# Reordering the loads of a fused attention and FFN block over two DMA queues

## The chip, the cores and the metric

One core of a Trainium2 chip runs the whole kernel. The metric is the device time of one execution in microseconds (us), lower is better. The core's engines are TensorE (PE, matmuls; PEld is its loading of weights), VectorE (DVE), ScalarE (ACT), GpSimd (POOL) and SyncE (SP). DMAs are issued from SP and ACT, each with its own queue; 16 DMA engines move the bytes of both.

## What is computed

x has 2048 rows of 512 in bf16; F is 1792; there are 32 heads of 16.

```python
xn = _layernorm(x, axis=-1)
return x + _A_ref(xn, A_wqkv, A_wo) + _B_ref(xn, B_w_gate, B_w_up, B_w_down)
# A: linear attention
q, k, v = heads of (xn @ wqkv)
phi = lambda t: jnp.where(t > 0, t + 1, jnp.exp(t)) + 1e-6
kv = einsum("bhsd,bhse->bhde", phi(k), v);  z = sum of phi(k) over s
o = (phi(q) @ kv) / (phi(q) . z + 1e-6);    A = o @ wo
# B: the FFN
B = (silu(xn @ w_gate) * (xn @ w_up)) @ w_down
```

## The kernel before

The rows are handled as 16 tiles of 128 rows (x0 to x15). Everything stays in SBUF: x, the normalized xn, its transpose xnT, and all weights.

First stage, tile by tile: statistics of x (`stat`, lines 277 to 303: two DVE instructions and two small ones, most on POOL), xn on DVE (`xn_dve`, line 285; tile 0 in two halves, line 328), the transpose of xn into xnT, then K's and Q's projections on PE (`proj`, line 365; tile 0 in halves of the contraction, `proj_half`, line 378), their exponentials on ScalarE (lines 401 to 411), K's features on DVE (`feat_k`: a clip, line 418, and a max-and-add from PSUM, line 427), and the accumulation of the features' transpose with xn (`gtacc`, line 460). Tiles 0 to 3 are transposed on PE (lines 340 and 312); tiles 4 to 15 by a DMA transpose on SP (`transpose_dma`, line 356), issued behind each tile's xn. K of tile t writes PSUM bank 2(t mod 2) and Q of tile t the bank after it, so K of tile 2 needs the bank of K of tile 0, which `feat_k(0)` reads last.

Second stage, FFN steps j = 0 to 55 (`ffn`, line 568): four matmuls with w_gate, four with w_up, Silu on ScalarE, a product on DVE. Between them stand `kvt` (reads w_v, line 666, after j = 1), `mmat` (reads w_o, line 689, after j = 3), the column sums z (`z_split`, `z_cols` with two DMA transposes, line 616, `z_sum`, line 623), the division by the attention's denominator, and from j = 17 on the output tiles (`outtile`), which read w_down (line 751).

The order of work on each engine is the order in which the program emits it, and it is written out by hand. `_Prog` derives the semaphore waits from named resources: an operation waits for the writers of what it reads. Every DMA has a semaphore of its own, and a DMA that must wait holds up everything behind it on its issuing queue. The weights of Q, K and V are one tensor of 512 rows; `wqkv_load(eng, h, name, i, c0, n)` (line 198) loads n row blocks of 128 (c0 to c0 + n - 1) of one of the three, and its name in the resources is (name, c0). `xload` (line 192) loads n tiles of x from t0. `wpiece` (line 211) loads one row block of w_gate or w_up (448 KB), `wload` (line 208) a whole weight.

Loads before, in the order of issue:

- SP: x0, x1, x2, K's blocks 0-1, Q's blocks 0-1, x4, x5, then, after Q's weights have landed, x6 to x9, x10 and x11, x12 to x15.
- ACT: K's blocks 2-3, x3, Q's blocks 2-3.
- SP, among the transposes: a piece of w_gate in each of the loop steps t = 2, 4, 6, 8 (line 539); w_up's four pieces, w_v and w_o at t = 11 (lines 541 to 544); w_down at t = 14 (line 546). xn of tiles 14 and 15, with their transposes, is emitted at t = 9.

PE starts with matmuls on a constant (`fill`, line 249), which have no result that is used.

Of the kernel before, what the change touches and what calls it, by code (L numbers as in the profile page):

```python
# [17 lines left out]
NDC = D // P  # L18
# [90 lines left out]
def bass_parallel_sum__linear_attn_block__swiglu_ffn__prompt_kernel(  # L109
# [13 lines left out]
    pe, act, dve, pool, sp = nc.tensor, nc.scalar, nc.vector, nc.gpsimd, nc.sync  # L123
    bf, f32 = dt.bfloat16, dt.float32

    with contextlib.ExitStack() as es:
        E = es.enter_context

        def sb(name, shape, d=bf):
            return E(nc.sbuf_tensor(name, [P] + shape, d))  # L130
# [3 lines left out]
        xnT = sb("xnT", [NDC, S])  # L134
        wqkv_sb = sb("wqkv_sb", [NDC, 3 * D])
        wo_sb = sb("wo_sb", [NG, D])
        wg_sb = sb("wg_sb", [NDC, F])
        wu_sb = sb("wu_sb", [NDC, F])
        wd_sb = sb("wd_sb", [NFC, D])
# [45 lines left out]
        def bk(i):  # L185
            return ("bank", i)
# [5 lines left out]
        def xload(eng, h, t0, n, after=()):  # L192
            K.dma(
                eng, lambda: h.dma_start(x_sb[:, t0:t0 + n, :], xv[:, t0:t0 + n, :]),
                r=list(after), w=[("x", t0 + i) for i in range(n)],
            )

        def wqkv_load(eng, h, name, i, c0, n):
            K.dma(
                eng,  # L200
                lambda: h.dma_start(
                    wqkv_sb[:, c0:c0 + n, i * D:(i + 1) * D],
                    A_wqkv[c0 * P:(c0 + n) * P, i * D:(i + 1) * D].rearrange("(c p) f -> p c f", p=P),
                ),
                w=[(name, c0)],
            )

        def wload(eng, h, name, dst, src):
            K.dma(eng, lambda: h.dma_start(dst[:, :, :], src.rearrange("(c p) f -> p c f", p=P)), w=[(name,)])

        def wpiece(name, dst, src, c):
            K.dma("sp", lambda: sp.dma_start(dst[:, c, :], src[c * P:(c + 1) * P, :]), w=[(name, c)])
# [1 line left out]
        K.op("pool", lambda: pool.memset(warm[:, :], 0.0), w=[("warm",)])  # L214
        K.op("act", lambda: act.activation(warm[:, :], warm[:, :], ACT.Exp), r=[("warm",)], w=[("warm",)])
        xload("sp", sp, 0, 1)
        xload("sp", sp, 1, 1)
        xload("sp", sp, 2, 1)
        wqkv_load("sp", sp, "wk", 1, 0, 2)
        wqkv_load("act", act, "wk", 1, 2, 2)  # L220
        xload("act", act, 3, 1)
        wqkv_load("sp", sp, "wq", 0, 0, 2)
        wqkv_load("act", act, "wq", 0, 2, 2)
        xload("sp", sp, 4, 1)
        xload("sp", sp, 5, 1)
        xload("sp", sp, 6, 4, [("wq", 0), ("wq", 2)])
        xload("sp", sp, 10, 2)
        xload("sp", sp, 12, 4)

# [8 lines left out]
            r=[("ident",)], w=[("ident",)],  # L238
# [16 lines left out]
        def masks():  # L255
            K.op("pool", lambda: pool.memset(maskt[:, :], 1.0), w=[("mask",)])
            mview = maskt[:, :].rearrange("p (a b) -> p a b", a=P // DH)
            K.op(
                "pool",
                lambda: pool.affine_select(  # L260
                    out=mview, in_=mview, compare_op=ALU.is_ge, fill=0.0,
                    base=0, pattern=[[-DH, P // DH], [0, DH]], channel_multiplier=1,
                ),
                r=[("mask",)], w=[("mask",)],
            )
            K.op(
                "pool",
                lambda: pool.affine_select(
                    out=mview, in_=mview, compare_op=ALU.is_ge, fill=0.0,
                    base=DH - 1, pattern=[[DH, P // DH], [0, DH]], channel_multiplier=-1,  # L270
                ),
                r=[("mask",)], w=[("mask",)],
            )
# [87 lines left out]
        def proj(t, b, lo, wname):  # L361
            K.op(
                "pe",
                [
                    (lambda c=c: pe.matmul(  # L365
                        banks[b], xnT[:, c, t * P:(t + 1) * P], wqkv_sb[:, c, lo:lo + D],
                        start=(c == 0), stop=(c == NDC - 1),
                    ))
                    for c in range(NDC)
                ],  # L370
                r=[("xnT", t), (wname, 0), (wname, 2)], w=[bk(b)],
            )

        def proj_half(t, b, lo, wname, h):
            K.op(
                "pe",
                [
                    (lambda c=c: pe.matmul(
                        banks[b], xnT[:, c, t * P:(t + 1) * P], wqkv_sb[:, c, lo:lo + D],
                        start=(c == 0), stop=(c == NDC - 1),  # L380
                    ))
                    for c in (2 * h, 2 * h + 1)
                ],
                r=[("xnTh", t, h), (wname, 2 * h)], w=[bk(b)],
            )

        def kb(t):
# [5 lines left out]
        def kproj(t):  # L393
            proj(t, kb(t), D, "wk")

        def qproj(t):
            proj(t, qb(t), 0, "wq")

        def exp_k(t):
            K.op(  # L400
                "act", lambda: act.activation(ek[:, t % NE, :], banks[kb(t)], ACT.Exp),  # L401
                r=[bk(kb(t))], w=[("ek", t % NE)],
            )

        def exp_q(t):
            K.op(
                "act", lambda: act.activation(eq[:, t, :], banks[qb(t)], ACT.Exp),
                r=[bk(qb(t))], w=[("eq", t)],
            )
            K.op(  # L410
                "act", lambda: act.activation(pkq[:, t, 1, :], banks[qb(t)], ACT.Copy),  # L411
                r=[bk(qb(t))], w=[("pq", t)],
            )
# [19 lines left out]
        def feat_k(t):  # L433
            e = t % NE
            clip(ek[:, e, :], ("ek", e))
            if t >= 2:
                zsum(t - 2, e)
            maxadd(pkq[:, t, 0, :], banks[kb(t)], ek[:, e, :], [bk(kb(t)), ("ek", e)], [("pk", t)])
# [17 lines left out]
        def gtacc(t):  # L456
            K.op(
                "pe",
                [
                    (lambda c=c: pe.matmul(  # L460
                        banks[4 + c], xn_sb[:, t, c * P:(c + 1) * P], pkq[:, t, 0, :],
                        start=(t == 0), stop=(t == NT - 1),
                    ))
                    for c in range(NDC)
                ],
                r=[("xn", t), ("pk", t)], w=[bk(4 + c) for c in range(NDC)],
            )

        def stat(t):
            bns(t)  # L470
            agg(t)
            rstd_pow(t)

        def xn(t):
            xn_dve(t)
            if t >= 4:
                transpose_dma(t)
# [49 lines left out]
        for t in range(2, NT):  # L527
            if t >= 3:
                kproj(t)
                exp_k(t)  # L530
                qproj(t)
                exp_q(t)
                feat_k(t)
            for i in STAT.get(t, ()):
                stat(i)
            for i in XN.get(t, ()):
                xn(i)
            if t in (2, 4, 6, 8):
                wpiece("wg", wg_sb, B_w_gate, t // 2 - 1)
            if t == 11:  # L540
                for c in range(NDC):
                    wpiece("wu", wu_sb, B_w_up, c)
                wqkv_load("sp", sp, "wv", 2, 0, 4)
                wload("sp", sp, "wo", wo_sb, A_wo)
            if t == 14:
                wload("sp", sp, "wd", wd_sb, B_w_down)
            if t == 12:
                masks()
            if t >= 3:
                gtacc(t - 2)  # L550
# [53 lines left out]
        def z_split():  # L604
            K.op("pool", lambda: pool.tensor_copy(zhi[:, :], zacc[:, :]), r=[("zacc",)], w=[("zhi",)])
            K.op(
                "pool",
                lambda: pool.tensor_tensor(out=zlo[:, :], in0=zacc[:, :], in1=zhi[:, :], op=ALU.subtract),
                r=[("zacc",), ("zhi",)], w=[("zlo",)],
            )  # L610

        def z_cols():
            for i, (src, name) in enumerate(((zhi, "zhi"), (zlo, "zlo"))):
                K.dma(
                    "sp",
                    lambda i=i, src=src: sp.dma_start_transpose(out=zT[:, i, :, :], in_=src[:, :]),
                    r=[(name,)], w=[("zT", i)],
                )
# [36 lines left out]
        def z_rows():  # L655
            K.op(
                "pool",
                lambda: pool.tensor_tensor(out=zb[:, :], in0=zrow[:, 0, :], in1=zrow[:, 1, :], op=ALU.add),
                r=[("zrow", 0), ("zrow", 1)], w=[("zb",)],
            )  # L660
# [125 lines left out]
            gt_evac(c)  # L786
        z_split()
        z_cols()
        NORM0 = 9
        PE_OUT = {3: 0, 6: 1, 9: 2, 12: 3}  # L790
        for j in range(NJ):
# [7 lines left out]
            if j == 4:  # L799
                z_sum()  # L800
            if j == NORM0 - 1:
                z_rows()
            if NORM0 <= j < NORM0 + 3 * NT:
                i, ph = (j - NORM0) // 3, (j - NORM0) % 3
                if ph == 0:
# [40 lines left out]
```

## Time and profile before

| what | us |
|---|---|
| median of three runs | 214.52 |
| the three runs | 214.17, 214.52, 217.59 |
| the profiled execution | 214.81 |
| its span (first to last instruction) | 213.6 |
| PE busy in the span | 207.7 |
| DVE, ACT, POOL busy | 119.2, 67.7, 72.6 |

The difference between the profiled execution and its span, 1.2 us, lies around the program. In a timeline each line has the start, the time, the engine, the line of the kernel, the operation, what is written and read, the tile's shape and how many instructions are merged; a bracket tells how long the engine was idle before it and which event ended that. Times are us from the start of the span. In the DMA view a line has what is loaded, the issuing queue, the number of issues, the KB of each and the median us from issue to landing; asked for a stretch with one issue in it, it gives that issue's own. The granted TensorE clock is full (1.00) in every stretch of the profile.

### The profile page before, as it was taken

Reading aid. Unit: us, or ns where it says so; the run is one execution under the profiler, and the core shown is the slowest. Engines: PE = TensorE matmul, PEld = TensorE weight load, DVE = VectorE, ACT = ScalarE, POOL = GpSimd, SP = SyncE. Lnnn points to the kernel's source line nnn. Section 1 sums busy time; section 2 is a strip of 40 time slices with the busy share of each in tenths; the row PEclk is TensorE's granted clock in tenths of the full one; section 3 lists DMA queues with packets and bytes.
Section 4 is the critical chain, followed back from the end, with each engine's and each line's share of the span. In section 5 each row is a group of like instructions: output and inputs, shape, how many; then the busy total and the mean of one; then the engine's idle time right before and its main releaser. Section 6 shows DMA issues by size and latency. Waiting matters only on the chain.

```text
span 213.6 us, 2768 instructions
## 1 busy us (share of the span) xinstructions
PE 207.7 (97%) x985; PEld 96.9 (45%) x1004; DVE 119.2 (56%) x240; ACT 67.7 (32%) x118; POOL 72.6 (34%) x95
## 2 busy tenths in 40 slices
PE   8799999999999999999999999999999999999995
PEld 4344434444544444444444444444444444444454
DVE  3799986333553777446373755464656536364121
ACT  2486666667363332213021302122132213121000
POOL 2538885549014344042130442121414131221100
PEclk9999999999999999999999999999999999999999
DMA  5784797997202011101101021101011010110101
GB/s 177 257 205 127 137 156 167 291 369 237 49 0 52 0 25 25 49 17 35 25 26 49 3 26 48 49 0 49 3 49 25 25 25 28 49 25 28 49 28 51
DMA packets 26271, 16.19 MB, mean 76 GB/s; under 512 B 18064, under 2 KB 24848, under 8 KB 26256
## 3 DMA queue, kind: packets, MB, share of 16 engines
q1 hardware_dynamic: 25568, 15.34, 28.5%
q10 hardware_dynamic: 688, 0.66, 1.0%
q8 instruction: 8, 0.13, 0.3%
q14 instruction: 7, 0.06, 0.1%
HBM read 9.70 MB, written 2.10 MB: 55 GB/s over the span
## 4 chain that ended last, share of the span: by engine, by line
PE 84%; issue 0%; DVE 0%
PE psum L568 45%; PE psum L751 23%; PE psum L740 6%; PE psum L365 6%; PE psum L460 4%; PE psum L666 0%; PE psum L689 0%; DVE out_sb L764 0%
## 5 line engine op out<-in xcount | busy, mean ns | idle before, releaser
L583 ACT ACTIVATE sg<-psum 128x512 bf16<-128x512 f32 x56 | 33.4, 598 | 106.8 <-PE psum L568 104.9
L568 PE MATMUL psum<-xnT,wu_sb 128*128 128x512 bf16 x222 | 57.4, 379 | 0.1
L568 PE MATMUL psum<-xnT,wg_sb 128*128 128x512 bf16 x217 | 56.0, 379 | 0.4
L698 POOL TENSOR_TENSOR prod<-pkq,zb 128x512 f32<-128x512 bf16 x16 | 18.6, 1161 | 57.8 <-DVE pkq L427 57.8
L568 PEld LDWEIGHTS psum<-xnT,wu_sb 128*128 128x128 bf16 x224 | 21.9, 98 | 26.4
L568 PEld LDWEIGHTS psum<-xnT,wg_sb 128*128 128x128 bf16 x224 | 21.9, 98 | 26.2
L764 DVE TENSOR_TENSOR out_sb<-psum,x_sb 128x512 bf16<-128x512 f32 (+1 forms) x17 | 11.2, 660 | 36.1 <-PE psum L751 36.1
L589 DVE TENSOR_TENSOR pkq<-psum,sg 128x512 bf16<-128x512 f32 x28 | 19.2, 687 | 18.6 <-PE psum L568 14.1
L722 POOL TENSOR_TENSOR pqn<-pkq,rden 128x512 bf16<-128x512 bf16 x16 | 16.9, 1055 | 36.6 <-DVE rden L716 36.6
L365 PE MATMUL psum<-wqkv_sb,xnT 128*128 128x512 bf16 x118 | 28.4, 379 | 0.5 <-ACT pkq L411 0.3
L589 DVE TENSOR_TENSOR xn_sb<-psum,sg 128x512 bf16<-128x512 f32 x28 | 18.8, 671 | 14.2 <-PE psum L568 13.6
L751 PE MATMUL psum<-wd_sb,xn_sb 128*128 128x512 bf16 (+1 forms) x124 | 25.6, 355 | 0.1
L751 PE MATMUL psum<-wd_sb,pkq 128*128 128x512 bf16 x110 | 25.4, 379 | 0.1
L452 POOL TENSOR_TENSOR zacc<-zacc,pkq 128x512 f32<-128x512 f32 x15 | 17.3, 1153 | 7.6 <-DVE ek L418 7.3
L365 PEld LDWEIGHTS psum<-wqkv_sb,xnT 128*128 128x128 bf16 x120 | 11.4, 98 | 14.4 <-ACT pkq L411 0.8
L751 PEld LDWEIGHTS psum<-wd_sb,xn_sb 128*128 128x128 bf16 x126 | 12.3, 98 | 11.9
L751 PEld LDWEIGHTS psum<-wd_sb,pkq 128*128 128x128 bf16 x112 | 11.0, 98 | 13.2
L740 PE MATMUL psum<-m_sb,eq 128*128 128x512 bf16 (+1 forms) x66 | 16.2, 366 | 0.1
L460 PE MATMUL psum<-pkq,xn_sb 128*128 128x512 bf16 x62 | 15.8, 379 | 0.1
L706 DVE TENSOR_REDUCE den<-prod 128x32 f32<-128x512 f32 x16 | 10.9, 684 | 5.7 <-POOL prod L698 5.7
L277 DVE BATCH_NORM_STATS2 stats<-x_sb 128x6 f32<-128x512 bf16 x16 | 10.9, 682 | 3.6 <-DMA x_sb<-in_A_x_dram 3.6
L401 ACT ACTIVATE ek<-psum 128x512 bf16<-128x512 f32 x16 | 9.6, 598 | 9.4 <-issue 4.1
(56 smaller groups left out, 131.4 us busy)
## 6 DMA issues: line engine op xcount, KB each, us to landing
out_dram<-out_sb SPq DMA_DIRECT2D x15, 128.0 KB, 1.7
wg_sb<-in_B_w_gate_dram SPq DMA_DIRECT2D x4, 448.0 KB, 4.2
wu_sb<-in_B_w_up_dram SPq DMA_DIRECT2D x4, 448.0 KB, 4.8
wd_sb<-in_B_w_down_dram SPq DMA_DIRECT2D x1, 1792.0 KB, 13.5
x_sb<-in_A_x_dram SPq DMA_DIRECT2D x2, 512.0 KB, 4.5
x_sb<-in_A_x_dram SPq DMA_DIRECT2D x5, 128.0 KB, 3.9
wqkv_sb<-in_A_wqkv_dram ACTq DMA_DIRECT2D x2, 256.0 KB, 4.0
wqkv_sb<-in_A_wqkv_dram SPq DMA_DIRECT2D x2, 256.0 KB, 5.5
```

What stands on the lines that cost most here:

```text
L277: K.op("dve", lambda: dve.bn_stats(stats[:, t, :], x_sb[:, t, :]), r=[("x", t)], w=[("st", t)])
L365: (lambda c=c: pe.matmul(banks[b], xnT[:, c, t * P:(t + 1) * P], wqkv_sb[:, c, lo:lo + D], start=(c == 0), stop=(c == NDC - 1),))
L452: lambda: pool.tensor_tensor(out=zacc[:, :], in0=zacc[:, :], in1=pk, op=ALU.add),
L460: (lambda c=c: pe.matmul(banks[4 + c], xn_sb[:, t, c * P:(c + 1) * P], pkq[:, t, 0, :], start=(t == 0), stop=(t == NT - 1),))
L568: (lambda c=c: pe.matmul(banks[b], w_sb[:, c, fc * P:(fc + 1) * P], xnT[:, c, C * 512:(C + 1) * 512], start=(c == 0), stop=(c == NDC - 1),))
L583: lambda: act.activation(sg[:, j % NSG, :], banks[gb], ACT.Silu),
L589: lambda: dve.tensor_tensor(out=hT(C, fc), in0=banks[ub], in1=sg[:, j % NSG, :], op=ALU.mult,),
L698: lambda: pool.tensor_tensor(out=p, in0=pkq[:, t, 1, :], in1=zb[:, :], op=ALU.mult),
L722: lambda: pool.tensor_tensor(out=pqn[:, t % NPN, :].rearrange("p (h e) -> p h e", e=DH), in0=pkq[:, t, 1, :].rearrange("p (h e) -> p h e", ...
L740: (lambda g=g: pe.matmul(dst, pqnT(t)[:, g, :], m_sb[:, g, lo:hi], start=(g == 0), stop=False,))
L751: (lambda fc=fc: pe.matmul(dst, hT(C, fc)[:, jj * P:(jj + 1) * P], wd_sb[:, fc, lo:hi], start=False, stop=(fc == NFC - 1),))
L764: lambda: dve.tensor_tensor(out=o, in0=src, in1=x_sb[:, t, lo:hi], op=ALU.add),
```

## The change

The first eleven loads are dealt over both queues in another order. SP: x0, x2, K's blocks 2-3, x3, Q's block 3, x4, and, after all of Q's weights have landed, x6 to x9, then x10 and x11, x12 to x15 as before. ACT: x1, K's blocks 0-1, Q's blocks 0-1, Q's block 2, x5. Q's blocks 2 and 3 are now two loads, so the readers of Q's weights wait for both. All pieces of w_gate, then w_up, w_v and w_o are issued at t = 9, behind the transposes of tiles 14 and 15. w_down is issued after z's two transposes.

```diff
         xload("sp", sp, 0, 1)
-        xload("sp", sp, 1, 1)
+        xload("act", act, 1, 1)
         xload("sp", sp, 2, 1)
-        wqkv_load("sp", sp, "wk", 1, 0, 2)
-        wqkv_load("act", act, "wk", 1, 2, 2)
-        xload("act", act, 3, 1)
-        wqkv_load("sp", sp, "wq", 0, 0, 2)
-        wqkv_load("act", act, "wq", 0, 2, 2)
+        wqkv_load("act", act, "wk", 1, 0, 2)
+        wqkv_load("sp", sp, "wk", 1, 2, 2)
+        wqkv_load("act", act, "wq", 0, 0, 2)
+        xload("sp", sp, 3, 1)
+        wqkv_load("act", act, "wq", 0, 2, 1)
+        wqkv_load("sp", sp, "wq", 0, 3, 1)
         xload("sp", sp, 4, 1)
-        xload("sp", sp, 5, 1)
-        xload("sp", sp, 6, 4, [("wq", 0), ("wq", 2)])
+        xload("act", act, 5, 1)
+        xload("sp", sp, 6, 4, [("wq", 0), ("wq", 2), ("wq", 3)])
         xload("sp", sp, 10, 2)
         xload("sp", sp, 12, 4)
...
-                r=[("xnT", t), (wname, 0), (wname, 2)], w=[bk(b)],
+                r=[("xnT", t), (wname, 0), (wname, 2)] + ([(wname, 3)] if wname == "wq" else []), w=[bk(b)],
...
-                r=[("xnTh", t, h), (wname, 2 * h)], w=[bk(b)],
+                r=[("xnTh", t, h), (wname, 2 * h)] + ([(wname, 3)] if wname == "wq" and h else []), w=[bk(b)],
...
-            if t in (2, 4, 6, 8):
-                wpiece("wg", wg_sb, B_w_gate, t // 2 - 1)
-            if t == 11:
+            if t == 9:
+                for c in range(NDC):
+                    wpiece("wg", wg_sb, B_w_gate, c)
                 for c in range(NDC):
                     wpiece("wu", wu_sb, B_w_up, c)
                 wqkv_load("sp", sp, "wv", 2, 0, 4)
                 wload("sp", sp, "wo", wo_sb, A_wo)
-            if t == 14:
-                wload("sp", sp, "wd", wd_sb, B_w_down)
...
         z_split()
         z_cols()
+        wload("sp", sp, "wd", wd_sb, B_w_down)
```

## The prediction

> **What bounds the kernel now.** I read the page's busy line first, then the chain that ended last, then the timeline of TensorE (PE) alone from the start to the FFN, then the stretches where that row of matmuls is broken: the timeline of all engines from 0 to 16 us, and the DMA issues one at a time with their time to landing.
>
> ```profile
> span 213.6 us, 2768 instructions
> PE 207.7 (97%) x985; PEld 96.9 (45%) x1004; DVE 119.2 (56%) x240; ACT 67.7 (32%) x118; POOL 72.6 (34%) x95
> ...
> PE 84%; issue 0%; DVE 0%
> ```
>
> PE is busy in 207.7 of 213.6 us, and the chain is PE from 30.43 us to the last tile. Only a hole between matmuls can be won, and only a new hole can be lost. The timeline of PE has two holes that data makes:
>
> ```profile
> 6.08 0.48 PE L249 MATMUL psum<-const-bfloat16-1.0 128*128 128x128 bf16 x4
> 7.73 1.02 PE L378 MATMUL psum<-wqkv_sb,xnT 128*128 128x512 bf16 x4 [1.17 <-DMA wqkv_sb<-in_A_wqkv_dram]
> 8.59 0.39 PE L312 MATMUL psum<-ident,xn_sb 128*128 128x128 bf16 x4
> 8.81 1.03 PE L378 MATMUL psum<-wqkv_sb,xnT 128*128 128x512 bf16 x4
> 9.68 1.03 PE L365 MATMUL psum<-wqkv_sb,xnT 128*128 128x512 bf16 x4
> ...
> 27.41 1.89 PE L365 MATMUL psum<-wqkv_sb,xnT 128*128 128x512 bf16 x8
> 29.14 1.03 PE L460 MATMUL psum<-pkq,xn_sb 128*128 128x512 bf16 x4
> 30.48 1.89 PE L365 MATMUL psum<-wqkv_sb,xnT 128*128 128x512 bf16 x8 [0.32 <-ACT pkq L411]
> ```
>
> Hole one: the first real projection, K of tile 0, starts at 7.73 us, 1.17 us after the last filler, and waits for K's weights. From there PE runs without a gap: groups of four matmuls follow each other every 0.86 us. Call 7.73 T0; whatever moves T0 moves the end.
>
> Hole two: the tile groups start every 2.59 us (24.82, 27.41), but the next at 30.48 instead of 30.00: 0.48 us lost. The row names ScalarE, but that write (Q of tile 8) is not what K of tile 9 needs. The DMA view shows what it needs, xn's transpose of tile 9, issued at 24.09 us behind a piece of w_gate at 23.13:
>
> ```profile
> 24.09 1.19 SPq L356 DMA_TRANSPOSE xnT<-xn_sb  x1
> ```
> ```profile
> xnT<-xn_sb SPq DMA_TRANSPOSE x1, 6.3
> ```
>
> 24.09 + 6.3 = 30.4, which is when PE goes on. Transposes with no weights ahead of them (issues at 14.05, 16.89, 21.89, 32.11) land in 2.4 us.
>
> **The start, part by part.** The first stage is a race of 1,792 KB. Landings before, each issue plus its own latency, with the KB that its queue had then delivered: SP x0 3.0 (128), x1 4.4 (256), x2 5.6 (384), K's rows c 0-1 7.6 (640), Q's c 0-1 8.26 (896), x4 8.6 (1,024), x5 9.0 (1,152); ACT K's c 2-3 4.0 (256), x3 5.2 (384), Q's c 2-3 6.7 (640). Between 4.0 and 6.7 us, both queues busy, ACT's moved 384 KB in 2.7 us; from 4.4 to 7.6 SP's moved 384 KB in 3.2.
>
> After, SP carries x0, x2, K's c 2-3, x3, Q's c 3, x4 (896 KB); ACT carries x1, K's c 0-1, Q's c 0-1, Q's c 2, x5 (896 KB). Same bytes, 11 issues in place of 10. The split of Q's second half adds one issue of about 0.45 us (those rows last 0.40 to 0.49) on ACT's queue, which has five now; they end near 3.3 us and ScalarE's first evacuation is at 6.06, so that is hidden. By position:
> - x1 first on ACT's queue: about 3.2 instead of 4.4.
> - K's c 0-1 at ACT's 384 KB: 5.2 instead of 7.6. K's c 2-3 at SP's 512 KB: 6.6 (halfway from 5.6 to 7.6).
> - Q's c 0-1 at ACT's 640: 6.7. x3 at SP's 640: 7.6 (before 5.2, so later by 2.4). Q's c 2 and 3, which end at 1,536 KB over both queues, where Q's c 0-1 stood before: 8.3. x4 among the last 256 KB: 8.9, between x4's 8.6 and x5's 9.0 before.
>
> Now the wait that takes over. T0 must satisfy:
> - the first xnT. Without K's weights PE is free at 6.56. VectorE (DVE) would do x1's statistics 0.33 us earlier, and the halves of xn(0) behind them, so 6.2 to 6.5.
> - K's c 2-3 are used 0.43 us after T0: 6.6 - 0.4 = 6.2.
> - Q's c 2 and 3 are first used 1.5 us after T0 (0.86 + 0.22 + 0.43): 8.3 - 1.5 = 6.8.
> - x3 and x4 sit in DVE's queue ahead of the features of tile 0:
>
> ```profile
> 8.65 0.69 DVE L277 BATCH_NORM_STATS2 stats<-x_sb 128x6 f32<-128x512 bf16 x1 [0.30 <-DMA x_sb<-in_A_x_dram]
> ...
> 9.38 0.18 DVE L280 BATCH_NORM_AGGREGATE mv<-stats 128x2 f32<-128x6 f32 x1
> ...
> 10.13 0.29 DVE L418 TENSOR_SCALAR ek<-ek 128x512 bf16<-128x512 bf16 x1 [0.57 <-ACT ek L401]
> ...
> 10.46 0.69 DVE L427 SCALAR_TENSOR_TENSOR pkq<-psum,ek 128x512 bf16<-128x512 f32 x1
> ```
>
> The reader is to see that DVE already waits 0.30 us for x4 here. The 0.57 us wait for K's exponential goes when T0 comes earlier. Then x4's landing plus 0.95 (statistics) plus 1.02 (clip to the end of line 427) is x4 + 2.0. K of tile 2 writes the same bank and starts 3.91 us after T0 (11.64 before): T0 is at least 8.9 + 2.0 - 3.9 = 7.0. x3's chain (0.69 + 0.1 + 0.41 to the end of xn(2), then x4's statistics, then the same 2.0) gives 7.6 + 3.2 - 3.9 = 6.9.
>
> So T0 becomes 7.0: a gain of 0.73 of the 1.17 us; late next is x4, with Q's last rows beside it. Bounds for x4: 8.57, if nothing but the same bytes counts (T0 6.66, gain 1.07); and 640 KB past x1's old place at SP's rate of 384 KB in 3.2 us, 4.4 + 5.3 = 9.7 (T0 7.8, a loss of 0.1). I take 8.9, since the total does not grow. The outer end, if x4 is no gate, is the first bullet's 6.4: gain 1.3. The wait ahead of x6's load now names Q's c 3 too; behind it on SP stand x10, x12 and the transpose of tile 4. Before, they were released at 8.2 to 8.3, as Q's weights landed: the same 8.3 now. x6 landed at 11.7 and was read past 13, so 1.3 us of cover.
>
> **The weights, part by part.** Moving four pieces of w_gate (issues of 0.58 us at 18.13, 23.13, 27.95, 33.34) behind the transposes gives hole two back: 0.48 us. [...]
>
> What it costs: w_gate (landed by 37.2, read at 50.1) joins one burst. In the burst of before, w_up's first piece was issued at 36.79 and landed after 3.9 us, and 10.3 pieces' worth (w_up, w_v, w_o, w_down) had landed by 53.6: 1.39 us a piece past the first. Now w_gate and w_up are first, eight pieces: 3.9 + 7 x 1.39 = 13.6 us after the first issue (12.1 at 1.17 a piece, 14.3 at 1.49, the fastest and slowest rows). That issue follows the transpose of tile 15, so it moves with PE, and so does the first read of w_up at 51.0: cover is 51.0 - 36.79 = 14.2 us. It fits by 0.6; I put nothing, at the slow end 0.1. w_v lands 1.5 later, 15.1, read at 53.6 (16.8); w_o 16.7 against 57.9 (21.1). w_down, issued behind z's two transposes near 54, takes at most its old 13.5 and is read at 83.8; if that cover were gone each us late would be one lost. z's transposes ran beside w_down before and still landed in 2.4. SP loses nothing: its issues are fewer between transposes.
>
> Sum: 0.73 + 0.48 = 1.2 us. The profiled execution took 214.81 us (span 213.6), 0.3 above the median of 214.52; its span should become 212.4, and the median 214.5 - 1.2 = 213.3.
>
> **The rivals.**
> - *The start gives nothing.* x3, Q's rows or x4 come so late that T0 stays at 7.6 to 7.9. For it: the 16 DMA engines are full from 2.5 to 7.5 us in both orders, and x3 is later by 2.4 us. Against: K's first rows jump from 7.6 to 5.2. Only hole two goes: 214.0.
> - *All of the start.* x4 lands before 8.3, T0 is 6.4: gain 1.33 + 0.48, 212.7. Against: x4's 8.57 before, with the same bytes ahead.
> - *w_up is late* (slower). It begins to cost when the eighth piece lands more than 14.2 us after the first issue and outweighs the 1.2 us gained past 15.4, which is 1.64 us a piece. At 1.9 us a piece it is 17.2: 3.0 lost, net 1.8 slower, 216.3. Against: no row of the old burst is over 1.49. For: it is the only cover under 1 us.
> - *The change does nothing to hole two*, because the transposes of tiles 9 to 11 hold each other (three in 2.5 us landed at 30.4, 30.7, 31.2): 213.8. It counts within the forecast's case.
>
> **How the numbers follow.** Forecast 0.62, nothing from the start 0.20, all of the start 0.11, w_up late 0.07. The forecast's own range is 212.9 to 214.0 (its x4 bounds with hole two in or out). Repeats lie 0.3 either side, so 212.4 to 214.7 takes in the second and third case too and leaves out the late w_up and some odd run. A measurement of this kernel can tell about 2% (4.3 us) from no change; no case here gains that, and w_up would need 2.2 us a piece to lose it: faster 0.02, same 0.94, slower 0.04.
>
> **What would show it.** Right: the first projection near 7.0 us or at 6.4 with small waits behind it; DVE's statistics of tile 3 and 4 waiting for x; groups every 2.59 us through tile 9; no transpose over 4 us after 18 us; no wait at the first w_up matmul. Wrong: x4 landing past 9.5 or before 8.3, a PE wait on a DMA near 49 us, or transposes of tiles 9 to 11 still landing late.

## The result, and the profile after

The changed kernel took 213.22 us (median of 13 runs, 212.96 to 214.0), the kernel before beside it 214.84 us (13 runs, 214.17 to 217.59). The ratio is 0.9928, 95% interval 0.9907 to 0.9948: 1.5 us faster, within 2%. The times of the kernel before fall in two groups, nine at 214.2 to 215.0 and four at 215.7 to 217.6 us, those of the changed kernel in one; the experiments take the second group up. The ratio is that of the means without the run at 217.59 us; against the lower group alone the mean of the changed kernel is 1.24 us lower.

The page of the profiled execution after (213.49 us) begins:

```profile
span 212.3 us, 2770 instructions
...
PE 207.1 (98%) x985; PEld 96.2 (45%) x1004; DVE 119.2 (56%) x240; ACT 68.0 (32%) x118; POOL 72.7 (34%) x95
```

The span is 1.3 us shorter. PE's timeline, the same rows as before:

```profile
6.46 1.02 PE L379 MATMUL psum<-wqkv_sb,xnT 128*128 128x512 bf16 x4
7.33 0.39 PE L313 MATMUL psum<-ident,xn_sb 128*128 128x128 bf16 x4
7.55 0.59 PE L379 MATMUL psum<-wqkv_sb,xnT 128*128 128x512 bf16 x2
8.42 0.59 PE L379 MATMUL psum<-wqkv_sb,xnT 128*128 128x512 bf16 x2 [0.28 <-DMA wqkv_sb<-in_A_wqkv_dram]
...
9.94 0.81 PE L366 MATMUL psum<-wqkv_sb,xnT 128*128 128x512 bf16 x3
11.08 1.02 PE L366 MATMUL psum<-wqkv_sb,xnT 128*128 128x512 bf16 x4 [0.33 <-DVE pkq L428]
...
13.03 1.03 PE L461 MATMUL psum<-pkq,xn_sb 128*128 128x512 bf16 x4
...
26.84 1.89 PE L366 MATMUL psum<-wqkv_sb,xnT 128*128 128x512 bf16 x8
...
29.43 1.89 PE L366 MATMUL psum<-wqkv_sb,xnT 128*128 128x512 bf16 x8
...
49.29 1.03 PE L567 MATMUL psum<-xnT,wg_sb 128*128 128x512 bf16 x4
50.20 1.02 PE L567 MATMUL psum<-xnT,wu_sb 128*128 128x512 bf16 x4
```

The first projection starts at 6.46 us, 1.27 earlier. Two waits give part of it back: Q's second half runs at 8.42 instead of 7.98 (0.44 lost), and K of tile 2 at 11.08 instead of 10.80 (0.28 lost), behind line 428 on DVE. At the first accumulation (13.03, before 13.59) 0.56 us is left. Hole two is gone: 26.84 and 29.43 are 2.59 apart, and K of tile 9 is 1.05 us earlier than before. At w_up 0.05 is lost (49.29 + 0.86 = 50.15, and the row says 50.20). The last instruction on DVE is 1.0 us earlier; the other 0.3 us of the span lies in the last output's DMA (1.9 us from issue to landing before, 1.6 here), which no term of the sum holds.

DVE in the same execution, where the bank of K of tile 2 comes free:

```profile
7.69 0.69 DVE L278 BATCH_NORM_STATS2 stats<-x_sb 128x6 f32<-128x512 bf16 x1 [0.76 <-DMA x_sb<-in_A_x_dram]
...
9.12 0.69 DVE L278 BATCH_NORM_STATS2 stats<-x_sb 128x6 f32<-128x512 bf16 x1 [0.23 <-DMA x_sb<-in_A_x_dram]
9.85 0.18 DVE L281 BATCH_NORM_AGGREGATE mv<-stats 128x2 f32<-128x6 f32 x1
9.95 0.26 DVE L419 TENSOR_SCALAR ek<-ek 128x512 bf16<-128x512 bf16 x1
10.24 0.69 DVE L428 SCALAR_TENSOR_TENSOR pkq<-psum,ek 128x512 bf16<-128x512 f32 x1
```

The brackets are the waits for x3 and x4; from x4's statistics to line 428 there is no gap left. Later on, xn of tiles 14 and 15, which stands ahead of the last transposes and the burst of weights, first in the kernel before, then after:

```profile
33.16 1.38 DVE L285 TENSOR_SCALAR xn_sb<-x_sb,mv,rstd 128x512 bf16<-128x512 bf16 x2
```
```profile
32.36 1.64 DVE L286 TENSOR_SCALAR xn_sb<-x_sb,mv,rstd 128x512 bf16<-128x512 bf16 x2
```

The DMA view of two issues, the transpose of tile 9 (at 23.87 us) and w_up's last piece (at 39.79):

```profile
xnT<-xn_sb SPq DMA_TRANSPOSE x1, 2.7
```
```profile
wu_sb<-in_B_w_up_dram SPq DMA_DIRECT2D x1, 448.0 KB, 10.3
```

The transpose lands 3.6 us sooner than before. w_up is complete at 50.1 us, when its first matmul is ready: no cover is left.

### The profile page after: what moved, and what is told of

The parts are those of the page before. It is cut to its first block, busy times and chain, and to the rows that moved or that the text cites. A ratio compares the mean times of both kernels' runs of the same rounds, so it can differ in the third digit from the quotient of the medians.

```text
span 212.3 us, 2770 instructions
## 1 busy us (share of the span) xinstructions
PE 207.1 (98%) x985; PEld 96.2 (45%) x1004; DVE 119.2 (56%) x240; ACT 68.0 (32%) x118; POOL 72.7 (34%) x95
## 4 chain that ended last, share of the span: by engine, by line
PE 94%; DMA 3%; SPq 1%; issue 1%; DVE 1%
PE psum L567 45%; PE psum L750 23%; PE psum L366 12%; PE psum L739 6%; PE psum L461 6%; DMA wqkv_sb<-in_A_wqkv_dram 3%; SPq L194 1%; PE psum L665 0%; PE psum L688 0%; DVE pkq L428 0%; PE psum L379 0%; SPq L201 0%; DVE out_sb L763 0%; DVE ek L419 0%; PE psum L313 0%
## 5 line engine op out<-in xcount | busy, mean ns | idle before, releaser
L567 PEld LDWEIGHTS psum<-xnT,wg_sb 128*128 128x128 bf16 x224 | 21.9, 98 | 26.2
L588 DVE TENSOR_TENSOR pkq<-psum,sg 128x512 bf16<-128x512 f32 x28 | 19.1, 686 | 18.2 <-PE psum L567 13.6
L588 DVE TENSOR_TENSOR xn_sb<-psum,sg 128x512 bf16<-128x512 f32 x28 | 18.8, 671 | 14.2 <-PE psum L567 13.6
L705 DVE TENSOR_REDUCE den<-prod 128x32 f32<-128x512 f32 x16 | 10.9, 684 | 5.9 <-POOL prod L697 5.9
L278 DVE BATCH_NORM_STATS2 stats<-x_sb 128x6 f32<-128x512 bf16 x16 | 10.9, 683 | 4.4 <-DMA x_sb<-in_A_x_dram 4.4
```

The source lines that it names most:

```text
L278: K.op("dve", lambda: dve.bn_stats(stats[:, t, :], x_sb[:, t, :]), r=[("x", t)], w=[("st", t)])
L567: (lambda c=c: pe.matmul(banks[b], w_sb[:, c, fc * P:(fc + 1) * P], xnT[:, c, C * 512:(C + 1) * 512], start=(c == 0), stop=(c == NDC - 1),))
L588: lambda: dve.tensor_tensor(out=hT(C, fc), in0=banks[ub], in1=sg[:, j % NSG, :], op=ALU.mult,),
```

## The experiments

**The new order of the first loads alone.** The edit takes the later weights back:

```diff
-            if t == 9:
-                for c in range(NDC):
-                    wpiece("wg", wg_sb, B_w_gate, c)
+            if t in (2, 4, 6, 8):
+                wpiece("wg", wg_sb, B_w_gate, t // 2 - 1)
+            if t == 11:
...
+            if t == 14:
+                wload("sp", sp, "wd", wd_sb, B_w_down)
...
-        wload("sp", sp, "wd", wd_sb, B_w_down)
```

> The new order of the first eleven loads alone; the later weights stay where they were before. Theory: the two parts are separate gains, the start about 0.55 us (the group of gtacc(0) at 13.0 us instead of 13.59) and the transposes' delay about 0.5 us. So here: against before 0.5 to 0.6 us faster (ratio 0.9975), K of tile 9 again late by 0.3 to 0.5 us behind a w_gate piece. Rival 1 (the gain is all of the start's): 1.1 to 1.5 us faster, with tiles 9 to 11 on time. Rival 2 (the start's gain is given back later): no difference to before.

213.23 us (6 runs; five at 212.9 to 213.5, the profiled one 214.65), ratio to before 0.9897 (0.986 to 0.9934). PE's timeline of the profiled execution:

```profile
6.35 0.61 PE L379 MATMUL psum<-wqkv_sb,xnT 128*128 128x512 bf16 x2
7.96 0.59 PE L379 MATMUL psum<-wqkv_sb,xnT 128*128 128x512 bf16 x2 [1.00 <-DMA wqkv_sb<-in_A_wqkv_dram]
...
27.36 1.89 PE L366 MATMUL psum<-wqkv_sb,xnT 128*128 128x512 bf16 x8
29.09 1.03 PE L461 MATMUL psum<-pkq,xn_sb 128*128 128x512 bf16 x4
30.65 1.89 PE L366 MATMUL psum<-wqkv_sb,xnT 128*128 128x512 bf16 x8 [0.54 <-ACT pkq L412]
```

Hole two is there, 0.70 us (27.36 to 30.65 instead of 29.95), with tile 9's transpose landing after 6.2 us: both as the theory of two separate parts says. But K's blocks 2-3 landed at 7.8 us in this execution against 6.6 in the one above, so its start gained nothing; and the other five runs gained 1.4 us on the lower group of the kernel before (median 214.63 in that batch), more than the theory's 0.55 and in the first rival's range. The size is a miss. None of the five was profiled, so hole two is shown for the slowest execution alone.

**The later weights alone.** The other half of the diff, on the old order of the first loads.

> The first loads as before; w_gate, w_up, w_v, w_o behind the last transpose, w_down behind z's transposes. Theory: 0.5 us faster than before (ratio 0.9977), the first projection at 7.7 us as before, groups every 2.59 us through tile 9, transposes of tiles 9 to 11 landing in under 3 us. Rival 1 (all of the gain is the start's): no difference to before, transposes 9 to 11 still landing after 30 us. A third reading: w_up's last piece lands after its first matmul is ready and takes part of the 0.5 us back.

214.78 us (12 runs), ratio 0.9987 (0.9953 to 1.002): unclear as a time. Its times keep both groups, seven at 214.2 to 214.8 and five at 215.9 to 216.6. PE's timeline:

```profile
7.66 1.02 PE L378 MATMUL psum<-wqkv_sb,xnT 128*128 128x512 bf16 x4 [1.19 <-DMA wqkv_sb<-in_A_wqkv_dram]
...
27.34 1.89 PE L365 MATMUL psum<-wqkv_sb,xnT 128*128 128x512 bf16 x8
...
29.93 1.89 PE L365 MATMUL psum<-wqkv_sb,xnT 128*128 128x512 bf16 x8
...
49.79 1.03 PE L566 MATMUL psum<-xnT,wg_sb 128*128 128x512 bf16 x4
50.84 1.02 PE L566 MATMUL psum<-xnT,wu_sb 128*128 128x512 bf16 x4
```

The first hole is as before, hole two is gone (0.48 us), and w_up's first matmul is 0.19 late (50.84 instead of 50.65): 0.3 us net in this execution, 0.2 between the medians of the lower groups (214.46 and 214.63). Here tile 9's transpose still took 4.6 us with no weights ahead of it, so a piece of w_gate is not all that can slow one. That the transposes of tiles 9 to 11 hold each other, as the fourth rival has it, is not shown: with the same spacing they landed after 2.7, 2.5 and 2.5 us in the changed kernel, where tile 7's took 4.0. Without a piece of w_gate they landed in time in both.

**w_up behind w_v and w_o.**

```diff
-                for c in range(NDC):
-                    wpiece("wu", wu_sb, B_w_up, c)
                 wqkv_load("sp", sp, "wv", 2, 0, 4)
                 wload("sp", sp, "wo", wo_sb, A_wo)
+                for c in range(NDC):
+                    wpiece("wu", wu_sb, B_w_up, c)
```

> The changed kernel with w_v and w_o issued ahead of w_up (the same bytes in the burst). Theory: the burst leaves w_up no cover (its last piece landed at 50.1 us, its first matmul ran at 50.2), so 1 MB ahead of it puts it 2.6 us later (w_v and w_o took 1.4 and 1.2 us) and PE waits 2.5 to 2.8 us before the first w_up matmul: 2.6 us slower than the changed kernel, 1.0 slower than before. Rival: w_up has cover that the profile hides, and then the time is that of the changed kernel within 0.5 us.

216.94 us (10 runs; four at 214.9 to 215.7, six at 216.8 to 218.1), ratio to before 1.0054 (1.0016 to 1.0091), the one kernel of these that is slower. PE's timeline:

```profile
52.38 1.02 PE L567 MATMUL psum<-xnT,wu_sb 128*128 128x512 bf16 x4 [2.51 <-DMA wu_sb<-in_B_w_up_dram]
```

The wait is 2.51 us, as expected, and the lower four runs (median 215.66) are 2.4 over the changed kernel: past its cover w_up cost PE one to one here. The slower rival of the prediction is real once w_up lands that late, and the changed kernel stands at its edge. The six runs another 2 us up all have a mean granted clock of 0.992, the other four of 1.000: the mark of the second group of times, below. The profiled execution is one of the four, so where the six lost it was not seen.

**Tile 4's statistics later on DVE.**

```diff
         xn_dve(2)
-        stat(4)
...
         feat_k(0)
         xn(3)
-        xn(4)
+        stat(4)
         stat(5)
+        xn(4)
```

> The changed kernel with the statistics of tile 4 emitted behind the features of tile 0 and xn of tile 3 on VectorE. Theory: the hole of 0.3 us ahead of K of tile 2 is x4's landing through VectorE's order, so it closes: gtacc(0) at 12.75 us instead of 13.03. Of this 0.28 us at the end as much is kept as w_up's landing allows: if the last transpose does not move with it, w_up's first matmul waits 0.2 to 0.3 us and the time is that of the changed kernel. Rival: the hole is Q's weights or the transposes, and then it stays at 0.3 us.

213.11 us (6 runs, 213.0 to 213.32), ratio 0.9882 (0.9848 to 0.9917). PE's timeline:

```profile
9.60 1.90 PE L366 MATMUL psum<-wqkv_sb,xnT 128*128 128x512 bf16 x7
11.34 0.39 PE L313 MATMUL psum<-ident,xn_sb 128*128 128x128 bf16 x4
...
12.42 1.04 PE L461 MATMUL psum<-pkq,xn_sb 128*128 128x512 bf16 x4
13.52 1.90 PE L366 MATMUL psum<-wqkv_sb,xnT 128*128 128x512 bf16 x8
```

The hole ahead of K of tile 2 is closed: x4 through DVE's order was its cause. Q's weights, the rival, are not: in the run with w_up last, which has the changed kernel's order on DVE, they came in time, and the hole is there:

```profile
10.64 0.38 PE L366 MATMUL psum<-wqkv_sb,xnT 128*128 128x512 bf16 x1 [0.26 <-DVE pkq L428]
```

A smaller hole opens ahead of K of tile 3 (13.52 instead of 13.28): its bank is now freed later, by line 428 on DVE, which ends at 13.46. The profiled execution is 0.5 us shorter than the changed kernel's (span 211.8), part of it from Q's weights, which came in time here; the medians differ by 0.1, no difference that these runs can tell.

**The first stage by itself.** To see the start without the rest, four kernels stop after the accumulation of tiles 0 to 3. What they leave out is told once, in the first expectation. The edit, on the kernel before and on the changed one:

```diff
-        STAT = {2: (7,), 3: (8,), 4: (9, 10), 5: (11,), 6: (12,), 7: (13,), 8: (14, 15)}
...
+        kproj(3)
+        exp_k(3)
+        qproj(3)
+        exp_q(3)
+        feat_k(3)
+        gtacc(1)
+        gtacc(2)
+        gtacc(3)
...
+            "sp", lambda: sp.dma_start(ov[:, :, :], x_sb[:, :, :]),
+            r=[("x", t) for t in range(NT)] + [("gt", c) for c in range(NDC)], w=[("res",)],
```

> The first stage of tiles 0 to 3 alone, with the loads of the kernel before: all of x and K's and Q's weights are loaded, tiles 0 to 3 are normalized, transposed on PE, projected, their features and the accumulation made; everything after is left out, and out is a copy of x, sent when the accumulation has been copied out. So its time moves one to one with PE's first stage. Theory: the first loads land up to 1 us later in some executions, so the times spread over 1 us or more, perhaps in two clusters (the kernel before has one at 214.3 to 214.9 and one at 215.9 to 216.5 us); first projection at 7.6 to 7.7 us in the faster. Rival: the clusters come from a later stage, and these times lie within 0.4 us.

> The same cut with the changed order of the first loads. Theory: 0.5 to 1.0 us faster than head_old's faster cluster, first projection near 6.5 us, then 0.2 to 0.7 us of waits for Q's block 3 and for the bank of tile 0. Rival: the order gains only in the profile shown, and the medians are equal within 0.2 us.

head_old: 27.6 to 27.9 us in four runs, 29.3 and 29.5 in two. head_new: 26.8 to 27.2 in five, 28.0 in one. The medians of the lower groups are 27.68 and 27.02: the order is worth 0.66 us where nothing else changes, and a second group of times, 1.6 us up, arises with the first stage alone.

> head_new with the statistics of tile 4 behind the features of tile 0 and xn of tile 3. Theory: the 0.2 to 0.3 us wait ahead of K of tile 2 goes, so 0.2 to 0.4 us faster than head_new. Rival: the wait moves to K of tile 3 (its bank is freed later, since tile 4's statistics now stand ahead of the features of tile 1) and the time is head_new's.

26.88 us (4 runs), against head_new's 27.05: 0.17, just under the theory's 0.2, and the ranges overlap (26.8 to 27.0 and 26.8 to 27.2).

For the next, the loads are head_new's, in the order of need, but all on SP:

```diff
-        xload("act", act, 1, 1)
+        xload("sp", sp, 1, 1)
...
-        wqkv_load("act", act, "wk", 1, 0, 2)
+        wqkv_load("sp", sp, "wk", 1, 0, 2)
```

> head_new with all eleven first loads issued from SP, in the order x0, x1, x2, K's blocks 0-1, 2-3, Q's 0-1, x3, Q's 2, Q's 3, x4, x5. It tells the order of need from the second queue. Theory (the order is what counts, the 16 engines are shared anyway): the waits after the first projection are no longer than head_new's, and the time is head_new's within 0.3 us. Rival (the second queue counts): one issue takes 0.4 to 0.5 us, so x4 is issued near 5.1 us instead of 3.2 and Q's block 3 near 4.7; both land later and the time is 0.3 to 1 us over head_new's.

27.05 us (4 runs, 26.9 to 27.1), the time of head_new. PE's timeline:

```profile
5.84 0.60 PE L371 MATMUL psum<-wqkv_sb,xnT 128*128 128x512 bf16 x2
6.60 0.59 PE L371 MATMUL psum<-wqkv_sb,xnT 128*128 128x512 bf16 x2 [0.16 <-DMA wqkv_sb<-in_A_wqkv_dram]
...
8.40 0.59 PE L371 MATMUL psum<-wqkv_sb,xnT 128*128 128x512 bf16 x2 [0.55 <-DMA wqkv_sb<-in_A_wqkv_dram]
```

The first projection is even 0.5 us earlier than head_new's 6.34 (x1 lands at 3.3 us), and Q's last block later (issued at 4.58, landed at 8.3). The second queue gave nothing that can be measured (27.05 us with it and without); the order did.

**The second group of times.** In the full kernels the group shows in the mean granted clock of an execution, which is 1.000 or 0.992. All 33 executions at 0.992 lie in an upper group: 22 of the kernel before in the batches of the experiments, five of the later weights alone, six with w_up last. Three upper ones of the kernel before read 1.000. A clock lower by 0.008 over 214 us is 1.7 us of full clock: about the distance of the groups (an estimate from these figures). No execution of the changed kernel, of the new order alone or with tile 4's statistics later (13, 6 and 6) is at 0.992. No full kernel was profiled at 0.992, so the place of the slow stretch was looked for in the first stage by itself, with three more kernels: head_old once more, head_old with fillers in the gap, and head_new with its small fillers removed.

```diff
         transpose_half(0, 5, 1)
         fill(4, P)
+        fill(18, P)
```
```diff
-        fill(6, P, [("mv", 0)])
-        fill(4, P, [("rstd", 0)])
         transpose_half(0, 4, 0)
         transpose_half(0, 5, 1)
-        fill(4, P)
```

> head_old once more, for a second profile and more times: 2 of its 6 times were 1.6 us over the other four (29.3 and 29.5 against 27.6 to 27.9 us). The pace of PE's first matmuls differs from one execution to the next: the spacing of 128x128 fillers falls from 0.11 to 0.06 us at 3.5 to 6.6 us in ten profiles. Theory (pace): in the later cluster PE is still at half pace after the 1 us gap ahead of the first projection, 0.43 us from matmul to matmul. Rival (late loads): its loads land 1 to 1.6 us later, as K's blocks 2-3 did once at 7.8 us. If the profile falls in the faster cluster, only the share of the times counts: about one third at 29.3 to 29.5.

27.6 to 27.9 us in three runs, 29.0 to 29.4 in three; the profiled one took 28.98. PE's timeline:

```profile
7.37 1.86 PE L370 MATMUL psum<-wqkv_sb,xnT 128*128 128x512 bf16 x4 [0.17 <-DMA wqkv_sb<-in_A_wqkv_dram]
9.03 0.63 PE L312 MATMUL psum<-ident,xn_sb 128*128 128x128 bf16 x4
9.45 1.37 PE L370 MATMUL psum<-wqkv_sb,xnT 128*128 128x512 bf16 x4
10.66 1.03 PE L357 MATMUL psum<-wqkv_sb,xnT 128*128 128x512 bf16 x4
```

K's blocks 0-1 had landed at 7.2 us, no later than in head_old (7.3), and the projection starts at 7.37 against 7.41. But its four matmuls take 1.66 us to the next group where head_old's take 0.86: 0.43 from one to the next in place of 0.22. In this execution the delay is PE at half pace, not late loads; the first accumulation comes at 14.56 instead of 13.27, 1.3 us later. But the gap ahead of the projection did not slow PE here: it is only 0.17 us, the fillers before it are 0.11 us apart, and PE reaches full pace for the first time past 10 us. In head_old PE was at full pace from 4.8 us, idled 0.99 us at the same place, and stayed at full pace, four matmuls in 1.02 us where head_old_2's took 1.86:

```profile
7.41 1.02 PE L370 MATMUL psum<-wqkv_sb,xnT 128*128 128x512 bf16 x4 [0.99 <-DMA wqkv_sb<-in_A_wqkv_dram]
```

> head_old with 18 more fillers of 128x128 behind tile 0's transposes, so that PE has work in most of the gap in which it waits for K's weights (18 take 1.0 us at full pace, 1.9 at half pace). Theory (pace): without the gap PE reaches full pace before the projection, and no time lies 1 us over the others. Rival (late loads): the later cluster stays, about a third of the times, 1.4 to 1.6 us over the rest; the faster cluster is 27.6 to 28.2 in both cases.

27.5 to 28.6 us in seven runs (median 28.05), none in a group of its own above 29. Of twelve runs of head_old five are at 28.98 or more, of these seven none: as the theory says, but with so few runs no more than a hint (the five would all fall among the twelve by chance once in 15 times). The profile doesn't settle it, since PE was at full pace from about 4 us, ahead of the added fillers. The lower end did not move. Of the spread of 1.1 us within the seven only 0.5 lies between first and last instruction (spans of 26.2 to 26.7 us; head_old's are 26.3 to 26.6 and 27.6 to 28.2); the rest lies around the program.

> head_new without the 14 small fillers (6, 4 and 4 of 128x128) around tile 0's normalization and transposes; the eight large ones stay, so PE idles from about 4.2 to 5.5 us and again to the first projection. Theory (pace): with the gap PE is at half pace in part or all of the first projections in some executions, and part of the times lie 1 to 1.7 us over head_new's 26.8 to 27.2. Rival: the fillers do not matter to the time, which is head_new's within 0.3 us.

27.8 to 29.0 us in six runs (median 28.16): 1.1 us over head_new. The profiled execution (29.03), first PE's timeline, then the windows view, in which PE's busy time follows the length of the stretch, and the figure behind POOL's busy time is the granted clock:

```profile
5.43 0.54 PE L341 MATMUL psum<-ident,xn_sb 128*128 128x128 bf16 x4 [1.17 <-DVE xn_sb L329]
6.19 0.60 PE L371 MATMUL psum<-wqkv_sb,xnT 128*128 128x512 bf16 x2 [0.22 <-ACT xnT L350]
7.66 1.01 PE L371 MATMUL psum<-wqkv_sb,xnT 128*128 128x512 bf16 x2 [0.87 <-DMA wqkv_sb<-in_A_wqkv_dram]
8.47 0.63 PE L313 MATMUL psum<-ident,xn_sb 128*128 128x128 bf16 x4
8.89 1.91 PE L371 MATMUL psum<-wqkv_sb,xnT 128*128 128x512 bf16 x4
```
```profile
4.05:7.46 3.41, 1.35 (x7) 0.34 (x6) 2.60 (x9) 0.66 (x2) 1.91 (x5) 1.00 1.02 349
7.70:9.00 1.30, 1.30 (x7) 0.75 (x8) 0.91 (x3) 0.00 (x0) 0.00 (x0) 0.50 0.12 42
9.00:10.00 1.00, 1.00 (x4) 0.35 (x3) 0.88 (x2) 0.86 (x2) 0.86 (x2) 0.50 0.29 49
```

PE had reached full pace (0.23 us between the two matmuls at 6.19), waited 0.87 us for K's blocks 2-3, and the granted clock fell to 0.50 within that wait, at 7.5 us, and rose again at 10.9. The wait alone is not shown to be the cause: PE had idled 1.17 us ahead of 5.43 as well and was busy for 1.35 us in all from 4.05 to 7.46, and single waits of 1.17 us (the kernel before), 1.19 (the later weights alone) and 1.00 (the new order alone) were followed by full pace (four matmuls in 1.02 us in the first two, two in 0.59 in the third, where the two at 7.66 here took 1.01). So in this execution idle PE time was followed by half pace, a loss beside the wait itself, and in those three it was not. In this execution those blocks were also late (7.5 us), so not all of its 2.0 us over head_new is pace. The other five runs, 0.8 to 1.3 us over head_new, were not profiled.

## Why the prediction was right

- *The size.* Predicted 213.3, measured 213.22, and that it is this close is luck. The kernel before has a median of 214.84 in 13 runs, 0.3 over the 214.52 that the prediction started from, and the medians are 1.6 us apart, 0.4 over the sum; the two misses cancel. The sum of 1.2 us stands against 1.5 by the ratio, 1.24 without the second group, and 1.0 on PE in the profile (0.56 + 0.49 - 0.05); the profiled spans differ by 1.3 because the last output's DMA adds 0.3.
- *The start.* Predicted to end at a shift of 0.73 us with x4 and Q's last rows as the next to be late; the profile has 0.56, with just these two waits. x4 was put at 8.9 and landed at 9.1, x3 at 7.6 and landed at 7.7, Q's last block at 8.3 and landed at 8.3. The method (a load's landing from its position in bytes) held for the late ones and failed for the early ones: K's blocks 0-1 landed at 6.33, not 5.2, x1 at 4.2, not 3.2, so DVE's first halves of xn came no earlier (5.25). Neither set the total, since the first xnT was ready only at 6.33 too and PE was held later by others. With x4 at 9.1 in place of 8.9 the prediction's own line gives 9.1 + 2.0 - 3.9 = 7.2, a shift of 0.5: the mechanism holds, the term was 0.2 too large. But this is one execution. The same first loads moved the first accumulation by 0.04, 0.56 and 1.01 us in three profiles (the new order alone 13.55, the changed kernel 13.03, w_up last 12.58), as K's blocks 2-3 landed at 7.8, 6.6 and 6.0. One landing time for each load stood for that whole spread, and that 0.73 lies inside it is partly luck. The upper bound of 1.07 passed over the prediction's own line for Q's rows (6.8, a gain of 0.93).
- *Hole two.* Predicted 0.48, measured 0.49, by the transposes' landing as stated: with the pieces of w_gate among them tile 9's landed after 6.3 and 6.2 us and PE waited, without them after 2.7 and 4.6 and it did not. Issuing the pieces ahead of the transposes did harm here, 0.48 us in the kernel before and 0.70 in the new order alone.
- *w_up.* The last piece was put at 13.6 us after the burst's first issue and landed at 13.8 (36.25 to 50.07). The step that failed is the cover: "That issue follows the transpose of tile 15, so it moves with PE." PE moved 1.05 us there, that transpose's issue only 0.54 (35.48 to 34.94), because it stands behind xn of tiles 14 and 15 on DVE. These started 0.80 us earlier but took 1.64 us instead of 1.38, as the two rows above show. The first w_up matmul of the kernel before stood at 51.20, not 51.0, so cover was 14.4 there and 13.9 after, not 14.2, and the price 0.05.
- *What was not seen.* A part of the gain by the ratio, 0.3 us, is not in the sum at all: the kernel before has the second group of times and the changed kernel's 13 runs do not. The prediction took 217.59 for an odd run and priced each wait at one to one. That the group goes with the old order of the first loads is shown by the counts (27 of 57 executions with the old order at a clock of 0.992, none of 25 with the new one, but for the kernel with w_up last); that the gap of 1.2 us ahead of the first projection makes it is the author's argument, and not shown. The six runs with w_up last, a kernel whose profile (at 1.000) has a wait of 2.51 us near 50 us in place of that gap, speak for idle time in general, which is not shown either: none of them was profiled.
- *Open.* By medians against the lower group the new order alone gained 1.4 us, the first stage by itself 0.66, the later weights 0.2, and both parts together no more than the order alone. The spread of the start (up to 1.0) and the last output's DMA go some way: it took 1.6 us in all four profiles of full kernels with the new order and 1.9 and 2.2 in the two with the old, though why is not shown. What hole two's 0.48 is worth at the end, with w_up at the edge of its cover, these runs don't settle; no second profile of the changed kernel or of the new order alone was taken. A burst made shorter by one early piece of w_gate, alone or together with the later statistics of tile 4, was not tried.

## What to carry to other kernels

Where one engine is busy from end to end, price a reordering of loads by writing down, for each tile, when its landing is needed and what stands in front of its reader on that reader's engine; the next limit may be another engine's order as well as a DMA (here 0.28 us behind DVE's order, 0.44 behind a DMA). When a burst is moved behind an event, ask what that event itself waits for: cover computed from the bound engine is wrong if the burst starts behind another one (here PE moved 1.05 us and the burst's first issue 0.54). In the first microseconds keep TensorE fed until the real work starts: without the small fillers the first stage took 28.16 us in place of 27.05, and in the one execution profiled idle time was followed by half pace (0.43 us from one matmul to the next), as it was not after waits of 0.99 to 1.19 us in four other profiles; so read several executions before a start is priced from one.

## What the runs showed of the hardware

PE's pace rose from half to full at 3.5 to 6.6 us in ten profiles of nearly the same start (128x128 fillers 0.11 us apart, then 0.06), and one execution, head_old_2's, was at half pace (matmuls 0.43 us apart in place of 0.22) to about 10 us. In head_new_nofill PE had gaps of 1.17, 0.22 and 0.87 us and was busy for 1.35 us from 4.05 to 7.46 us; from 7.5 to 10.9 us the granted clock was 0.50. In head_old_2 the clock row shows 1.00 where the matmuls are 0.43 us apart, and so does that of the kernel before, where fillers are 0.11 us apart up to 6.3 us; at the start the spacing has to be read, not the row.
